# Moving the q casts of the later batches from ScalarE to GpSimd in a fused retention and MLP kernel

## The chip, the cores and the metric

The kernel runs on one core of a Trainium2 chip. The metric is the device time of one execution in microseconds (us). Each core has five engines with a queue of their own: TensorE (PE in the profile; PEld is its weight load), VectorE (DVE), ScalarE (ACT), GpSimd (POOL) and SyncE (SP, which here only issues DMAs). Batches are counted from 0, and a stage is named by the batch whose MLP runs in it.

## The reference, cut to what matters

Retention (a decayed linear attention, 4 batches, 8 heads, 768 positions, 64 per head) is followed by a Fourier mix, a normalization and a two-layer MLP with a residual.

```python
for t in range(S):                       # retention
    state = gamma * state + outer(k[:, :, t], v[:, :, t])
    y[:, :, t] = scale * q[:, :, t] @ state
x = y.transpose(0, 2, 1, 3).reshape(B, S, H * D)
u = x + real(fft(fft(x, axis=1), axis=2))
un = (u - mean(u)) / sqrt(var(u) + 1e-6)
out = u + relu(un @ w_ch1) @ w_ch2       # 512 -> 2048 -> 512
```

## The kernel before

The kernel does retention in chunks, two heads (a pair) at a time, four pairs per batch. It is a software pipeline: while the MLP of batch b runs on PE, the attention of batch b+1 is slipped in between its matmuls. For batches 2 and 3 each pair needs casts of q, k and v to fp16; q and k are then transposed by DMA. Before the change q is cast on ScalarE, k and v on GpSimd:

```python
def cast_unit(b, i):                     # batch b, pair i
    ...
        q16 = qzs[i % 2]                 # two q16z buffers, used in turn
        for h2 in range(2):
            dst = q16[:, h2, :, D * h2:D * h2 + D]
            nc.scalar.copy(dst, q32[:, h2])
    for h2 in range(2):
        kc = nc.gpsimd.tensor_scalar(out=kd[:, :, h2, :], in0=k32[:, h2],
                                     scalar1=gkd[...], scalar2=1.0, ...)
    last_cast[b, i] = nc.gpsimd.tensor_scalar(out=v16, in0=v32..., scalar1=1.0, scalar2=1.0, ...)
def t_unit(b, i):
    ...
    nc.sync.dma_start_transpose(qT, q16_of[b, i])   # q16z is free again when this has read it
    nc.sync.dma_start_transpose(kT, kd_of[b, i])
```

Beside the casts GpSimd has one more duty: it adds the residual x to u, per block of 128 rows, and VectorE's statistics (bn_stats, tile bst) wait for that:

```python
def s2_unit(b, kb):                      # row block kb of batch b, 0 to 5
    ...                                  # VectorE writes u from PSUM (pq) and qn
    nc.gpsimd.tensor_tensor(out=u[:, kb, 0:256], in0=u[:, kb, 0:256], in1=x..., op=ALU.add)
    nc.gpsimd.tensor_tensor(out=u[:, kb, 256:512], ...)
    nc.vector.bn_stats(bst, u[:, kb, :]) # then bn_aggr, and un on ScalarE
```

The MLP's first layer makes 16 row groups of psh in three PSUM buffers, which it shares with the second layer's psc. ScalarE or VectorE empties each psh into ht, by a list:

```python
def h_unit(b, rt, fb):
    psh = ps_pm.tile(...)                # three buffers
    ... four matmuls ...
    if fb in ACT_ROWS[rt]:
        nc.scalar.activation(ht16[:, fb, :], psh, AF.Relu, ...)
    else:
        nc.vector.tensor_scalar(out=ht16[:, fb, :], in0=psh, ...)
```

The other PSUM tiles of this phase share a pool of five buffers: wkA (q times k), wkK (v times k, for the state), wkY (the attention's output), pq (the Fourier mix) and pst (transposes of un).

Of the kernel before, what the change touches and what calls it, by code (L numbers as in the profile page):

```python
# [12 lines left out]
ALU = mybir.AluOpType  # L13
# [6 lines left out]
B, H, S, D = 4, 8, 768, 64  # L20
# [10 lines left out]
ON_ACT = {'q': (0, 1, 0), 'kv': (1, 1, 1), 'g': (0, 1, 1), 'gr': (0, 0, 0)}  # L31
FB = 1
NPE = 2
ACT_ROWS = ((2, 4, 5, 6, 7, 8, 9, 10, 14), (0, 3, 6, 7, 9, 10, 11, 12, 14, 15))


@with_exitstack
def kernel(
# [9 lines left out]
    nc = tc.nc  # L48
# [149 lines left out]
    for h in range(H):  # L198
# [4 lines left out]
                            scalar2=float(math.log(0.125)), op0=ALU.mult, op1=ALU.add)  # L203
    nc.vector.tensor_scalar(out=gexp[:, 1], in0=lgrow, scalar1=icol[:, 5:6], scalar2=None,
                            op0=ALU.mult)
    nc.scalar.activation(gexp, gexp, AF.Exp, bias=0.0, scale=1.0)
    for h2 in range(2):
# [10 lines left out]
                            scalar1=float(np.float32(1.0 / S)), scalar2=None, op0=ALU.mult)  # L218
    nc.vector.tensor_scalar(out=icoln[:, 3:5], in0=icol[:, 3:5], scalar1=float(1.0 / DM),
                            scalar2=None, op0=ALU.mult)  # L220
# [134 lines left out]
    def cast_unit(b, i):  # L355
        def run():
            h0 = 2 * PAIR_ORDER[i]
            q32, k32, v32 = (in_of.pop((n, b, i)) for n in "qkv")
            kd = kp.tile([P, NCH, 2, D], f16, tag="kd16", name="kd16")
            v16 = vp.tile([P, NCH, 2, D], f16, tag="v16", name="v16")  # L360
            with ExitStack() as es:
                if b < NPE:
                    if (b, i - 1) in last_cast:
                        es.enter_context(tc.issue_after(last_cast[b, i - 1].ins))
                    q16 = qzs[i % 2].rearrange("p h c d -> p (h c d)")[
                        :, 0:NCH * P].rearrange("p (c h d) -> p c h d", c=NCH, h=2)
                    es.enter_context(tc.issue_after(nc.gpsimd.tensor_scalar(
                        out=q16, in0=q32.rearrange("p h c d -> p c h d"), scalar1=1.0,
                        scalar2=1.0, op0=ALU.mult, op1=ALU.mult).ins))
                else:  # L370
                    q16 = qzs[i % 2]
                    for h2 in range(2):
                        dst = q16[:, h2, :, D * h2:D * h2 + D]
                        nc.scalar.copy(dst, q32[:, h2])
                for h2 in range(2):
                    kc = nc.gpsimd.tensor_scalar(out=kd[:, :, h2, :], in0=k32[:, h2],  # L376
                                                 scalar1=gkd[:, h0 + h2:h0 + h2 + 1],
                                                 scalar2=1.0, op0=ALU.mult, op1=ALU.mult)
                    if b < NPE:
                        es.enter_context(tc.issue_after(kc.ins))  # L380
                last_cast[b, i] = nc.gpsimd.tensor_scalar(
                    out=v16, in0=v32.rearrange("p h c d -> p c h d"), scalar1=1.0, scalar2=1.0,
                    op0=ALU.mult, op1=ALU.mult)
            q16_of[b, i], kd_of[b, i], v16_of[b, i] = q16, kd, v16
        return run
# [538 lines left out]
    def h_unit(b, rt, fb):  # L924
        def run():
            unT = lb[b]["unT"]
            psh = ps_pm.tile([P, 384], f32, tag="pm", name="psh", padded_shape=[P, DM])
            for cb in range(4):
                nc.tensor.matmul(psh, w116[:, cb, fb * P:(fb + 1) * P],  # L929
                                 unT[:, cb, rt * 384:(rt + 1) * 384],  # L930
                                 start=(cb == 0), stop=(cb == 3))
            if fb in ACT_ROWS[rt]:
                nc.scalar.activation(ht16[:, fb, :], psh, AF.Relu, bias=0.0, scale=-1.0)  # L933
            else:
                nc.vector.tensor_scalar(out=ht16[:, fb, :], in0=psh, scalar1=-1.0, scalar2=0.0,  # L935
                                        op0=ALU.mult, op1=ALU.max)
        return run
# [239 lines left out]
```

## Time and profile before

| | before |
|---|---|
| time, median of 4 runs (3 were known at the prediction, 249.08) | 248.9 us |
| span of the profiled run | 247.3 us |
| PE busy | 233.9 us (95%) |
| PE idle between 85 and 185 us | 2.4 us |
| stage of batch 1, first psh to first psc matmul | 95.02 to 109.04: 14.02 us |
| stage of batch 2, the same | 147.14 to 162.69: 15.55 us |

A stage holds the first half of the MLP's first layer and the casts and attention of the next batch, and both stages do the same work. So a stage's length, read from PE's timeline, shows a stall or a delay directly, with less noise than the time of a whole run; what noise is left, up to 0.4 us, is seen in batch 3's casts alone below.

### The profile page before, as it was taken

To read this page: it belongs to the slowest core of one execution; us is meant where nothing else is said; L and a number is where in the kernel's file an instruction comes from. 1 tells how busy PE (TensorE), PEld (TensorE's weight loads), DVE (VectorE), ACT (ScalarE), POOL (GpSimd) and SP (SyncE) were. 2 spreads that over 40 slices of the span, in tenths; PEclk is the share of its full clock that TensorE was granted. 3 is DMA by queue.
4 is the path that set the end of the run, shared out by engine and by line. 5 is a ranking of instruction groups with operands and counts; after the bars stand their busy time and mean duration, and the time that the engine had idled before them with its cause. 6 is when DMAs were issued, how large, how long until landed. Compare 5 with 4: busy or idle time off the path is not lost.

```text
span 247.3 us, 5310 instructions
## 1 busy us (share of the span) xinstructions
PE 233.9 (95%) x2024; PEld 144.0 (58%) x2024; DVE 176.2 (71%) x427; ACT 130.8 (53%) x295; POOL 73.7 (30%) x130
## 2 busy tenths in 40 slices
PE   6897899999999999999999999799999998999994
PEld 2454668956776645655567446465666455545543
DVE  8988957898788786995985738687895656424112
ACT  8798678487786437862247427742247317202500
POOL 6668500385500074660000717530001305000000
PEclk9999999999999999999999999999999999999999
DMA  8998999699999388999999479595200241221012
GB/s 174 259 257 142 200 197 205 155 248 260 271 229 211 55 170 182 202 168 162 226 265 210 102 156 201 111 127 130 87 1 3 44 150 21 45 85 42 0 45 85
DMA packets 99209, 36.39 MB, mean 147 GB/s; under 512 B 89840, under 2 KB 96240, under 8 KB 99184
## 3 DMA queue, kind: packets, MB, share of 16 engines
q1 hardware_dynamic: 94960, 31.86, 63.3%
q0 software_dynamic: 4224, 4.19, 10.5%
q8 instruction: 16, 0.26, 0.4%
q14 instruction: 9, 0.07, 0.1%
HBM read 27.26 MB, written 6.29 MB: 136 GB/s over the span
## 4 chain that ended last, share of the span: by engine, by line
PE 68%; DVE 10%; ACT 7%; POOL 4%; DMA 4%; SPq 3%; issue 2%; POOLq 0%; ACTq 0%; DVEq 0%
PE psc L972 30%; PE psh L929 20%; PE ps L729 3%; SPq L159 3%; PE psh L946 3%; DMA k<-in_k_dram 2%; PE wkA L593 2%; DMA qTz<-q16z 2%; DVE bst L882 2%; POOL u L865 2%; PE wkY L647 2%; ACT un L884 1%; DVE u L833 1%; PE wkY L643 1%; POOL u L863 1%
## 5 line engine op out<-in xcount | busy, mean ns | idle before, releaser
L972 PE MATMUL psc<-w,ht 128*128 128x512 f16 (+1 forms) x400 | 89.8, 370 | 0.0
L929 PE MATMUL psh<-unT,w 128*128 128x384 f16 x448 | 82.1, 326 | 2.3 <-ACT ht L933 2.2
L972 PEld LDWEIGHTS <-ht 128*128 128x128 f16 x400 | 38.0, 98 | 35.0
L929 PEld LDWEIGHTS <-w 128*128 128x128 f16 x448 | 42.2, 98 | 26.1 <-issue 3.3
L933 ACT ACTIVATE ht<-psh 128x384 f16<-128x384 f32 x67 | 31.9, 489 | 37.2 <-PE psh L929 36.2
L863 POOL TENSOR_TENSOR u<-u,x 128x256 f32<-128x256 f32 x21 | 13.3, 635 | 110.7 <-DVE u L833 100.3
L976 DVE SCALAR_TENSOR_TENSOR ob<-psc,stats,u 128x512 f32<-128x512 f32 (+1 forms) x25 | 18.0, 721 | 26.5 <-PE psc L972 26.4
L935 DVE TENSOR_SCALAR ht<-psh 128x384 f16<-128x384 f32 x45 | 24.7, 550 | 8.7 <-PE psh L929 8.2
L596 DVE TENSOR_TENSOR atm<-wkA,maskp 128x512 f16<-128x512 f32 x36 | 23.9, 682 | 1.0 <-PE wkA L593 1.0
L884 ACT ACTIVATE un<-u,stats 128x512 f16<-128x512 f32 x21 | 15.2, 723 | 15.2 <-DVE stats L883 10.9
L882 DVE BATCH_NORM_STATS2 bst<-u 128x6 f32<-128x512 f32 x21 | 14.6, 694 | 8.9 <-POOL u L865 8.8
L622 DVE SCALAR_TENSOR_TENSOR s<-s,gk,wkK 128x128 f16<-128x128 f16 x48 | 16.5, 343 | 2.5 <-ACT s L618 1.4
L655 ACT ACTIVATE x<-wkY,gexp 128x384 f16<-128x384 f32 x24 | 12.9, 584 | 8.3 <-PE wkY L647 8.3
L145 PE MATMUL wps<-ht 128*128 128x512 f16 x40 | 12.8, 422 | 2.2 <-POOL ht L196 2.2
L376 POOL TENSOR_SCALAR kd<-k,gexp 128x384 f16<-128x384 f32 x24 | 13.8, 585 | 2.2 <-DMA k<-in_k_dram 2.2
L865 POOL TENSOR_TENSOR u<-u,x 128x256 f32<-128x256 f32 x21 | 13.3, 635 | 3.6 <-DVE stats L883 1.8
L593 PE MATMUL wkA<-qTz,kT 128*128 128x256 f16 x72 | 13.6, 273 | 0.3 <-ACT x L655 0.2
L828 ACT COPY qn<-pq 128x128 f32<-128x128 f32 x18 | 4.9, 273 | 12.9 <-PE pq L826 12.9
L946 PE MATMUL psh<-unT,w 128*128 128x128 f16 x192 | 11.5, 219 | 0.1
L946 PEld LDWEIGHTS <-w 128*128 128x128 f16 x192 | 11.0, 98 | 0.7 <-issue 0.5
L833 DVE SCALAR_TENSOR_TENSOR u<-pq,g,qn 128x256 f32<-128x256 f32 x18 | 8.5, 474 | 3.1 <-ACT qn L829 2.8
L593 PEld LDWEIGHTS <-kT 128*128 128x128 f16 x72 | 6.7, 98 | 6.7 <-issue 0.9
(164 smaller groups left out, 319.1 us busy)
## 6 DMA issues: line engine op xcount, KB each, us to landing
q<-in_q_dram SPq DMA_DIRECT2D x16, 384.0 KB, 6.2
k<-in_k_dram SPq DMA_DIRECT2D x16, 384.0 KB, 5.6
v<-in_v_dram SPq DMA_DIRECT2D x16, 384.0 KB, 6.2
out_dram<-ob SPq DMA_DIRECT2D x23, 256.0 KB, 2.5
w<-in_moe_w_ch_dram POOLq DMA_DIRECT2D x8, 512.0 KB, 11.0
out_dram<-ob SPq DMA_DIRECT2D x2, 128.0 KB, 1.7
unT<-un SPq DMA_TRANSPOSE x15, 2.4
kT<-kd SPq DMA_TRANSPOSE x8, 3.1
```

What stands on the lines that cost most here:

```text
L593: mm = nc.tensor.matmul(wk[:, c2], st["kT"][:, c, :], st["qT"][:, :, c, :], start=True, stop=True)
L596: nc.vector.tensor_tensor(out=st["atm"][:, 2 * part:2 * part + 2], in0=wk, in1=maskp[:, PAIR_ORDER[i]].unsqueeze(1).to_broadcast([P, 2, 2, ...
L622: nc.vector.scalar_tensor_tensor(out=s16[:, c], in0=s16[:, c - 1], scalar=gk2[:, hp:hp + 1], in1=wk[:, c - c0], op0=ALU.mult, op1=ALU.add)
L865: nc.gpsimd.tensor_tensor(out=u[:, kb, 256:512], in0=u[:, kb, 256:512], in1=x[:, kb, 1, 257:1:-1], op=ALU.add)
L882: nc.vector.bn_stats(bst, u[:, kb, :])
L884: una = nc.scalar.activation(un, u[:, kb, :], AF.Identity, bias=stats[:, kb, 0:1], scale=-1.0)
L929: nc.tensor.matmul(psh, w116[:, cb, fb * P:(fb + 1) * P], unT[:, cb, rt * 384:(rt + 1) * 384], start=(cb == 0), stop=(cb == 3))
L933: nc.scalar.activation(ht16[:, fb, :], psh, AF.Relu, bias=0.0, scale=-1.0)
L935: nc.vector.tensor_scalar(out=ht16[:, fb, :], in0=psh, scalar1=-1.0, scalar2=0.0, op0=ALU.mult, op1=ALU.max)
L946: mm = nc.tensor.matmul(psh[:, f], w116[:, cb, fb * P:(fb + 1) * P], unT[:, cb, kb * P:(kb + 1) * P], start=(cb == 0), stop=(cb == 3))
L972: nc.tensor.matmul(psc[:, c0:c1], ht16[:, fb, rb3 * P:(rb3 + 1) * P], w216[:, fb, c0:c1], start=(fb == 0), stop=(fb == NFB - 1))
L976: nc.vector.scalar_tensor_tensor(out=ob[:, c0:c1], in0=psc[:, c0:c1], scalar=lb[b]["st"][:, rb, 3:4], in1=lb[b]["u"][:, rb, c0:c1], op0=AL ...
```

## The change

The intent: all casts of a pair stand in one queue, ScalarE is left to empty PSUM, and GpSimd, busy only 30%, takes the work.

```diff
-ACT_ROWS = ((2, 4, 5, 6, 7, 8, 9, 10, 14), (0, 3, 6, 7, 9, 10, 11, 12, 14, 15))
+ACT_ROWS = ((2, 4, 5, 6, 7, 8, 9, 10, 14), (0, 3, 6, 7, 9, 10, 11, 12, 14, 15), (2, 4, 5, 6, 7, 8, 9, 10, 14))
...
                         dst = q16[:, h2, :, D * h2:D * h2 + D]
-                        nc.scalar.copy(dst, q32[:, h2])
+                        nc.gpsimd.tensor_scalar(out=dst, in0=q32[:, h2], scalar1=1.0,
+                                                scalar2=1.0, op0=ALU.mult, op1=ALU.mult)
...
-            if fb in ACT_ROWS[rt]:
+            if fb in ACT_ROWS[2 if (b, rt) == (B - 1, 0) else rt]:
```

## The prediction

> **What bounds the kernel now.** I read the page first: how full TensorE (PE) is, and where.
>
> ```profile
> PE 233.9 (95%) x2024; PEld 144.0 (58%) x2024; DVE 176.2 (71%) x427; ACT 130.8 (53%) x295; POOL 73.7 (30%) x130
> PE   6897899999999999999999999799999998999994
> POOL 6668500385500074660000717530001305000000
> ```
>
> PE is busy 233.9 of 247.3 us. The missing 13.4 us lie mostly at the start and after the last matmul, so the table of busy time by stretch is needed: from 85 to 185 us, which holds everything the change touches, PE misses 0.49 us (85 to 100), 0.26 (100 to 115), 1.54 (145 to 160) and 0.09 (160 to 175), together 2.4 us or 1%. No change of casts can win more. GpSimd (POOL) has room on average (30%), but its strip has two crowded spells, near 87 to 110 and 140 to 163 us. The view of waits for PE between 85 and 185 us names the holes:
>
> ```profile
> PE psh L929 <- ACT ht L933: 1.5, 1, 1.5
> PE pst L913 <- ACT un L884: 0.4, 1, 0.4
> PE wkA L593 <- ACT x L655: 0.2, 1, 0.2
> ```
>
> One wait of 1.5 us is most of it: a matmul of the first MLP layer (psh) needs a PSUM buffer that ScalarE (ACT) has not emptied. The chain of work that ended last says why, and the timeline of ACT shows it directly:
>
> ```profile
> 150.85 5.25 DMA qTz<-q16z
> 156.20 0.17 ACT q16z L374
> 157.05 0.40 ACT q16z L374
> 157.45 0.39 ACT ht L933
> ```
>
> ```profile
> 156.20 0.51 ACT L374 CAST q16z<-q 128x384 f16<-128x384 f32 x1 [1.96 <-DMA qTz<-q16z]
> ```
>
> There are two q16z buffers. The cast of batch 3's fourth pair stands early in ACT's queue, and may not write its buffer before the transposing DMA of the second pair has read it, at 156.1. For 1.96 us ACT stands still, with PSUM to empty behind it, and PE stops:
>
> ```profile
> 155.92 0.44 PE L612 MATMUL wkK<-v,kd 128*128 128x128 f16 x5
> 157.90 0.81 PE L929 MATMUL psh<-unT,w 128*128 128x384 f16 x4 [1.54 <-ACT ht L933]
> ```
>
> The casts of batch 2 (counted from 0) run beside batch 1's MLP from 95 us on, those of batch 3 beside batch 2's from 147; below I name the stage by the MLP's batch. The earlier stage runs the same sequence without that stall: from the first psh matmul (95.02 and 147.14) to the second layer's first matmul (109.04 and 162.69) it takes 14.02 there and 15.55 here, 1.53 us more.
>
> **What the Trainium skill says.** "PSUM — Partial Sum Buffer", section "Engine vs sequencer instructions": the queues of ScalarE, VectorE and GpSimd are strict FIFO. The ACT stall agrees. "ScalarE: Activation LUTs", section "What ACT_TABLE_LOAD costs": an instruction with immediate scale and bias takes 186 ns + 0.833 ns per element, 506 ns for 384; the trace has 509 for the median q cast. "Perfetto Trace Analysis", section "GPSIMD Engine Instruction": GpSimd spans are unreliable, take the spacing of starts. I do so below; k casts listed at 1.15 us a pair are spaced 1.11. "GPSIMD Engine Reference", section "1. Specifications": GpSimd shares SBUF interfaces with VectorE, which contends in some forms. No number in this trace shows that, so I give it only width.
>
> **The change, part by part.** The third row list is a decoy: (2, 4, 5, ... 14) for the last batch's first half equals the list used now. The instruction order confirms it: PE's sequence is identical in both kernels. Value 0.
>
> Removed: 16 casts from ACT, 16 x 509 ns = 8.1 us of ACT's 130.8. ACT isn't the bound; what counts is the stall, 1.54 us of PE.
>
> Added: 16 casts on POOL. The nearest row is the k cast of the same shape and strides (585 ns, spacing 1.11 us for two), so 8 pairs x 1.11 = 8.9 us, POOL from 73.7 to about 83. That alone costs nothing. Where they stand does: in each pair q comes first, then k and v, and the residual additions of the next row block (u) follow in the same FIFO. POOL now, after batch 1's fourth row block:
>
> ```profile
> 98.20 0.64 POOL L865 TENSOR_TENSOR u<-u,x 128x256 f32<-128x256 f32 x1
> 98.82 1.15 POOL L376 TENSOR_SCALAR kd<-k,gexp 128x384 f16<-128x384 f32 x2
> 99.93 0.83 POOL L381 TENSOR_SCALAR v<-v 128x768 f16<-128x768 f32 x1
> 100.73 0.63 POOL L863 TENSOR_TENSOR u<-u,x 128x256 f32<-128x256 f32 x1
> 101.32 0.63 POOL L865 TENSOR_TENSOR u<-u,x 128x256 f32<-128x256 f32 x1
> ```
>
> There is no gap: with q in front, the additions of the fifth row block start at 101.84 and end near 103.1 instead of 101.95. VectorE (DVE) takes them at once, as its timeline shows, and it too is a FIFO:
>
> ```profile
> 102.01 0.68 DVE L882 BATCH_NORM_STATS2 bst<-u 128x6 f32<-128x512 f32 x1
> 105.70 0.54 DVE L935 TENSOR_SCALAR ht<-psh 128x384 f16<-128x384 f32 x1
> 106.86 0.55 DVE L935 TENSOR_SCALAR ht<-psh 128x384 f16<-128x384 f32 x1
> ```
>
> So the statistics move from 102.01 to about 103.13, and everything on DVE behind them, which is nearly gapless, by 1.12 us. That includes two evacuations of psh (rows 11 and 12 of 16), for which PE waits three rows later:
>
> ```profile
> 106.99 0.81 PE L929 MATMUL psh<-unT,w 128*128 128x384 f16 x4
> 107.85 0.81 PE L929 MATMUL psh<-unT,w 128*128 128x384 f16 x4
> ```
>
> Row 14 needs row 11's buffer, now free at 106.24, 0.75 us before. In the new DVE order one state update (spacing about 0.3 us) also steps ahead of that evacuation: it starts at 105.70 + 1.12 + 0.35 = 107.2 and ends at 107.75, so row 14 starts 0.8 us late. Row 12 follows after 0.47 for the evacuation and 0.62 for two updates, at 108.3 to 108.85; row 15 starts at 108.9, and the second layer, 0.87 us later, at 109.77 instead of 109.04: **+0.73 us** for batch 1.
>
> For batch 2 the stall goes, but the same delay comes in. Additions of the fifth block end at 155.38 instead of 154.27, the statistics start at 155.42; with batch 1's spacings the next u starts at 156.70, the next statistics at 158.49, row 11 is emptied at 159.51 to 160.05, row 14 starts at 160.1, row 15 at 161.2, the second layer at 162.07 instead of 162.69: **-0.62 us**.
>
> The other deadlines hold. Fourth-pair casts on POOL end near 112 and 164.6 (now 108.9 and 162.7), and the matmuls on that k and v come at 116.8 and 170.5. Their transposes are read at 121.2 and 174.9. Second pair in batch 1: k's transpose is issued 0.3 us later (102.4), read at 107.1, before row 14, so not in addition. Sum: +0.73 - 0.62 = **+0.1 us**, 249.2.
>
> **Rivals.**
> A, the pure gain: DVE and three PSUM buffers absorb POOL's delay, only the stall goes: 249.1 - 1.5 = 247.5. For it: the stall is certain to go from ACT, and ACT has 8 us less to do. Against: no gap on POOL ahead of the fifth block, and slack of only 0.75 us on row 11 against 1.5 us of delay.
> B, POOL becomes the local bound in both batches and transposes shift too: k's transpose of the second pair lands after 4.6 us already now, at 106.7 with PE right behind it, and one k load moves some 3 us later into that spell. Two losses of 1 us and a smaller gain: 250.3.
> C, the wait for the q16z buffer returns on POOL and holds k and v of the fourth pair. Against: by my times that cast starts after 109 and 159.7, its buffer is read out by 105 and 158. Worth 0.
>
> **Range and chances.** I give my sum about two thirds and A most of the rest: 0.65 x 249.2 + 0.25 x 247.5 + 0.1 x 250.3 = 248.9 us. From A with a little less (247.3) to B: 247.3 to 250.3. A gain of 2% would be 5 us, more than the 2.4 us that PE misses in the region; a loss of 2% needs several new stalls as large as the old one. Chances: faster 0.01, within 2% 0.97, slower 0.02.
>
> **What would show it.** Right: PE's wait of 1.5 us on ACT near 156 is gone; ACT is near 123 us busy, POOL near 83, its q casts as long as k casts; DVE waits about 1.1 us for POOL ahead of the fifth block's statistics (near 102 and 154.3); PE waits for DVE's ht near 107 and 159, under 1 us each. From psh to the second layer it takes about 14.8 us in both batches. Wrong, step by step: no PE wait on DVE there means A, and the delay was absorbed; a longer wait on k's transpose means B; a q cast on POOL much longer than 585 ns, or slower DVE instructions beside it, means that the two contend. A time below 247 or above 251 us would contradict the whole account.

## The result, and the profile after

The changed kernel takes 248.98 us (median of 4 runs, 248.76 to 249.18), the kernel before 248.9 (4 runs). The ratio is 1.0001, with a 95% interval of 0.9982 to 1.0019. Ratios here are the mean time of one kernel's runs over that of the other's runs of the same rounds, so they are not quite the ratio of the medians.

The page of the changed kernel, the same lines as shown of before (busy time of each engine, then busy tenths of PE and GpSimd in 40 slices):

```profile
PE 234.4 (95%) x2024; PEld 144.2 (58%) x2024; DVE 176.5 (71%) x427; ACT 124.8 (50%) x279; POOL 81.6 (33%) x146
PE   6797899999999999999999999999999998999994
POOL 7668500385500075690000636760002314000000
```

The work has moved: ACT lost 6.0 us of busy time, POOL gained 7.9. PE's strip has lost its 7 of the 26th slice (near 157 us), where the stall was, and is at 9 throughout from the sixth slice to the 33rd. Now the waits of PE between 85 and 185 us (engine, line and tile waited for: total us, times, longest):

```profile
PE wkY L644 <- DVE u L837: 0.8, 2, 0.4
PE pst L914 <- ACT un L885: 0.4, 1, 0.4
```

The 1.5 us wait on ScalarE is gone, and a new one has come that was not there: twice 0.4 us on VectorE's u. In the stage of batch 2 ScalarE no longer stops for the q16z buffer (it does wait 1.64 us for VectorE's statistics, before un at 157.23). Its timeline:

```profile
153.52 1.23 ACT L934 ACTIVATE ht<-psh 128x384 f16<-128x384 f32 x3
154.63 0.29 ACT L829 COPY qn<-pq 128x128 f32<-128x128 f32 x1
```

Before, the qn copy that follows these three evacuations came 3.6 us after their start (153.01 and 156.62), behind the stuck cast; now it comes 1.1 us after. So the stall is gone. What took the gain back shows in the chain of work that ended last, in the stage of batch 1 (start, duration, what; "..." marks what is left out):

```profile
99.79 1.13 POOL kd L377 x2
100.92 0.80 POOL v L382
101.73 0.60 POOL u L864
...
102.95 0.69 DVE bst L883
...
108.15 0.48 DVE ht L936
...
108.67 0.81 PE psh L930 x4
```

The chain now runs from GpSimd's casts over the additions and VectorE's statistics to a PSUM evacuation and into PE. Each link is the FIFO of one engine. The two groups on VectorE between 94 and 165 us that tell it, of before and then of the changed kernel (count | busy us, mean ns of one | idle before, ended by):

```profile
L882 DVE BATCH_NORM_STATS2 bst<-u 128x6 f32<-128x512 f32 x9 | 6.2, 692 | 3.2 <-POOL u L865 3.2
L596 DVE TENSOR_TENSOR atm<-wkA,maskp 128x512 f16<-128x512 f32 x18 | 12.0, 681 | 0.4 <-PE wkA L593 0.4
```

```profile
L883 DVE BATCH_NORM_STATS2 bst<-u 128x6 f32<-128x512 f32 x9 | 6.2, 694 | 5.0 <-POOL u L866 5.0
L597 DVE TENSOR_TENSOR atm<-wkA,maskp 128x512 f16<-128x512 f32 x18 | 12.0, 682 | 0.4 <-PE wkA L594 0.4
```

VectorE's instructions are no slower beside the added GpSimd work (692 and 694, 681 and 682 ns). It only waits 1.8 us longer for the additions, 0.9 in each stage. GpSimd's and VectorE's timelines give the size of the link: the q casts sit right ahead, and the statistics start at 102.95 where they had started at 102.01.

```profile
98.80 0.99 POOL L374 TENSOR_SCALAR q16z<-q 128x384 f16<-128x384 f32 x2
99.77 1.15 POOL L377 TENSOR_SCALAR kd<-k,gexp 128x384 f16<-128x384 f32 x2
```

```profile
102.95 0.69 DVE L883 BATCH_NORM_STATS2 bst<-u 128x6 f32<-128x512 f32 x1 [0.86 <-POOL u L866]
104.61 0.48 DVE L837 SCALAR_TENSOR_TENSOR u<-pq,g,qn 128x256 f32<-128x256 f32 x1
106.99 0.53 DVE L936 TENSOR_SCALAR ht<-psh 128x384 f16<-128x384 f32 x1
108.07 0.55 DVE L936 TENSOR_SCALAR ht<-psh 128x384 f16<-128x384 f32 x1
```

On PE, first in the stage of batch 1, then once in that of batch 2:

```profile
105.14 0.43 PE L644 MATMUL wkY<-s,qTz 128*128 128x64 f16 x9 [0.42 <-DVE u L837]
...
107.57 0.81 PE L930 MATMUL psh<-unT,w 128*128 128x384 f16 x4
...
157.97 0.44 PE L644 MATMUL wkY<-s,qTz 128*128 128x64 f16 x9 [0.42 <-DVE u L837]
```

PE first stops at wkY, whose PSUM buffer the late u frees at 104.61 + 0.48 = 105.09. Then row group 14 starts 0.05 us after VectorE has emptied row 11 (106.99 + 0.53 = 107.52), and row 15 starts at 108.67 (the chain's last line above), 0.05 us after row 12 is emptied (108.62). These two waits are real, too, though the view of waits does not list them. The stages now take 95.00 to 109.54 = 14.54 us and 147.64 to 162.36 = 14.72 us: +0.52 in the first, -0.83 in the second, -0.3 together, against a time that did not change within its noise (the rest of the span is 0.2 us longer).

### The profile page after: what moved, and what is told of

It is laid out like the page before. It is cut to its first block, busy times and chain, and to the rows that moved or that the text cites. A ratio compares the mean times of both kernels' runs of the same rounds, so it can differ in the third digit from the quotient of the medians.

```text
span 247.2 us, 5308 instructions
## 1 busy us (share of the span) xinstructions
PE 234.4 (95%) x2024; PEld 144.2 (58%) x2024; DVE 176.5 (71%) x427; ACT 124.8 (50%) x279; POOL 81.6 (33%) x146
## 4 chain that ended last, share of the span: by engine, by line
PE 66%; DVE 10%; POOL 8%; ACT 6%; SPq 3%; issue 2%; DMA 2%; POOLq 0%; DVEq 0%; ACTq 0%
PE psc L973 30%; PE psh L930 19%; PE ps L730 3%; SPq L159 3%; PE psh L947 3%; DVE bst L883 3%; POOL u L866 2%; DMA k<-in_k_dram 2%; POOL u L864 2%; PE wkA L594 2%; PE wkY L648 2%; DVE u L834 1%; DVE ht L936 1%; PE wkY L644 1%; PE tq L550 1%
## 5 line engine op out<-in xcount | busy, mean ns | idle before, releaser
L594 PE MATMUL wkA<-qTz,kT 128*128 128x256 f16 x72 | 13.6, 273 | 0.0
L382 POOL TENSOR_SCALAR v<-v 128x768 f16<-128x768 f32 x12 | 10.0, 833 | 2.0 <-DMA v<-in_v_dram 1.9
```

The costliest lines, as they stand in the source:

```text
L594: mm = nc.tensor.matmul(wk[:, c2], st["kT"][:, c, :], st["qT"][:, :, c, :], start=True, stop=True)
```

## The experiments

My theory is that two things of about the same size cancel. (1) In the stage of batch 2 the fourth pair's cast, waiting in ScalarE's queue for a buffer, costs some 1.5 us. (2) The second pair's q cast on GpSimd delays the additions of the fifth row block, and through VectorE's FIFO and the PSUM buffers it costs both stages. Rivals: the gain was hidden and nothing costs anything; GpSimd's added work costs in proportion, by contention or by sheer load; ScalarE's load, not its wait, is what mattered; VectorE's new instruction order is the loss. In all kernels PE's instructions stand in the same order; each result was correct. The order on ScalarE, casts aside, is not the same everywhere, and no run takes it apart: in batch 1's stage of the kernel before, of pair 2 alone and of batch 3's casts alone, the first emptying of wkY into x stands behind un and starts at 107.9 to 108.4 us; in all the others it stands ahead of un, at 104.9 to 106.9. In batch 2's stage the order is the same in all.

All runs together; "stage" is from the first psh to the first psc matmul in the profile, "rest" the span less both stages:

| run | time, median of 6 (of 4 for before, changed) | batch 1's stage | batch 2's stage | rest | ratio to before, 95% |
|---|---|---|---|---|---|
| before | 248.9 | 14.02 | 15.55 | 217.7 | |
| changed | 248.98 | 14.54 | 14.72 | 217.9 | 1.0001 (0.9982 to 1.0019) |
| pairs 3 and 4 on GpSimd | 247.21 | 13.91 | 13.73 | 217.5 | 0.9904 (0.9869 to 0.9940) |
| pair 2 alone | 249.51 | 14.35 | 15.88 | 217.7 | 0.9998 (0.9962 to 1.0034) |
| third buffer, casts on ScalarE | 247.40 | 13.55 | 13.61 | 217.9 | 0.9908 (0.9870 to 0.9946) |
| batch 2's casts alone | 248.91 | 14.52 | 15.04 | 217.5 | 0.9979 (0.9942 to 1.0016) |
| all but pair 2 on GpSimd | 246.99 | 13.57 | 13.75 | 217.5 | 0.9909 (0.9886 to 0.9931) |
| pair 2 cast twice | 251.62 | 15.70 | 15.88 | 217.7 | 1.0099 (1.0074 to 1.0125) |
| batch 3's casts alone | 248.71 | 14.38 | 14.70 | 217.6 | 0.9973 (0.9947 to 1.0000) |
| row list put back | 249.13 | 14.51 | 14.70 | 218.0 | 0.9995 (0.9972 to 1.0018) |

The rest stays within about 0.5 us everywhere, so differences larger than that lie in the two stages. The kernel before, run along, had medians of 249.62 (11 runs, 248.51 to 251.84) and 249.16 (248.37 to 250.29); differences of a few tenths are read from the stages, not from the ratios. I count pairs from 1 in this section; the code and the records' names count them from 0.

### Pairs 3 and 4 on GpSimd, pairs 1 and 2 on ScalarE

```diff
+                        if i >= 2:
                             nc.gpsimd.tensor_scalar(out=dst, ...)
+                        else:
+                            nc.scalar.copy(dst, q32[:, h2])
```

> Only the q casts of the third and fourth head pair go to GpSimd; those of the first and second stay on ScalarE. My theory (the stall of 1.5 us comes from the fourth pair's cast waiting in ScalarE's queue, the loss from the second pair's cast standing ahead of the fifth block's additions on GpSimd): both stages run without PE waits over 0.3 us, 14.0 us from the first psh to the first psc matmul in each, and the time is 248.9 - 1.5 = 247.4 us. Rival (GpSimd's extra work costs in proportion, whichever pair it is): half of the change's loss stays, some 248.4 us. Rival (the stall was hidden anyway): 248.9.

Measured 247.21 us, 13.91 and 13.73 us. Half of the casts moved, and the time is below the 247.4 of my theory and the proportional rival's 248.4. The stall wasn't hidden: without it and without the delay the time falls. Against the kernel before in the same rounds the gain is 2.4 us (0.9904), more than the 1.5 expected: the kernel before ran slower in these rounds (249.62) than its 248.9, and, as the third buffer shows below, its stage of batch 1 was not clean either.

### Pair 2 alone on GpSimd

The condition is `i == 1` instead of `i >= 2`.

> Only the second pair's q cast goes to GpSimd. My theory: the fifth block's additions are delayed by 0.97 us as in the changed kernel; in batch 1's stage PE loses about 0.5 us (14.5 instead of 14.0 us); in batch 2's stage the old stall of 1.5 us stays and covers the delay; 248.9 + 0.5 = 249.4 us. Rival (cost in proportion to GpSimd's work): a quarter of the loss, 249.15. Rival (the loss comes from the new order of VectorE's instructions, which this kernel does not have): 14.0 us in batch 1's stage and 248.9.

Measured 249.51 us. The ratio cannot resolve 0.5 us, since before's own runs scattered that day. The profile can. PE's waits between 85 and 185 us have both causes at once:

```profile
PE psh L933 <- ACT ht L937: 1.8, 2, 1.5
PE wkY L647 <- DVE u L840: 0.4, 1, 0.4
```

The wkY wait comes with this one pair, and with VectorE's instructions in before's order, so the new order is not its cause. Batch 1's stage is 14.35 us, 0.33 longer, less than the 0.5 expected. In batch 2's stage I had expected the stall to cover the delay; it did not quite, 15.88 instead of 15.55. The trace says why. The second pair's cast on GpSimd ends later, so its transpose is issued at 152.33 instead of 150.85, and the fourth pair's cast on ScalarE gets its buffer at 156.73 instead of 156.20:

```profile
152.33 1.43 SPq L545 DMA_TRANSPOSE qTz<-q16z  x1
156.73 0.51 ACT L378 CAST q16z<-q 128x384 f16<-128x384 f32 x1 [2.29 <-DMA qTz<-q16z]
```

That is 0.53 us later, in a stage that began 0.20 us later (147.34): the 0.33 us. The run also shows that two casts fewer in ScalarE's queue do not remove the stall: PE still waits 1.45 us at 158.01.

### A third q16z buffer, all q casts on ScalarE

From the kernel before, not the changed one. The third buffer lies in part of a table that only batch 0 reads; the middle lines are the loop that zeroes the buffers' padding.

```diff
+    qzs.append(gk5[:, 1:4].rearrange("p n e c -> p (n e c)").bitcast(f16)[
+        :, 0:2 * NCH * P].rearrange("p (h c d) -> p h c d", h=2, c=NCH))
...
-        for j in range(2):
+        for j in range(3):
...
-                    q16 = qzs[i % 2]
+                    q16 = qzs[(0, 1, 0, 2)[i]]
```

> All q casts stay on ScalarE as before, but the fourth pair's goes to a third q16z buffer (in memory that only batch 0 uses), so that it has no transpose to wait for. My theory (the wait, not ScalarE's 8 us of casts, cost the 1.5 us): no ScalarE wait on the transpose, stages of 14.0 and about 14.1 us, 247.4 us. Rival (ScalarE's load is what held PE): the stage of batch 2 keeps over 15 us and the time stays at 248.9.

Measured 247.40 us. That this is the expected number to the digit is luck: the two stages are 0.9 us shorter than I had expected, and against the kernel before in the same rounds the gain is 2.3 us (0.9908) and not 1.5. ScalarE keeps all of its 16 casts and its wait on the transpose is gone, and both stages are the shortest of all with 13.55 and 13.61 us. The edit moved something else too: with its own buffer the fourth pair's cast stands much earlier in ScalarE's queue (143.58 us instead of 156.20), so the stage of batch 2 holds two casts less. That this load is not what mattered is shown by pair 2 alone, where two other casts left the same stage and the stall stayed. Together the two runs show that the wait for the buffer cost the time in batch 2's stage. This also corrects my ruler: batch 1's 14.02 us before was not clean, an undisturbed stage takes about 13.6. How much of that half microsecond is ScalarE's order (x behind un) and how much the landing of transposes is not shown.

### Batch 2's casts alone on GpSimd

The condition is `b == 2`.

> Only batch 2's q casts go to GpSimd (they run beside batch 1's MLP, where there was no stall to remove); batch 3's stay on ScalarE. My theory: loss without gain, batch 1's stage 14.5 us, batch 2's 15.5 as before, 249.4 us. Rival (the change costs nothing by itself and its gain is hidden too): 248.9.

Measured 248.91 us, a miss by 0.5. The first half of the expectation holds: batch 1's stage takes 14.52 us. But batch 2's fell from 15.55 to 15.04 with its casts on ScalarE as before. The stall itself, from PE's timeline, is shorter than the 1.54 us of before, and the times of the second pair's transpose and of the fourth pair's cast behind it say how:

```profile
151.28 1.48 SPq L545 DMA_TRANSPOSE qTz<-q16z  x1
155.94 0.51 ACT L378 CAST q16z<-q 128x384 f16<-128x384 f32 x1 [1.45 <-DMA qTz<-q16z]
157.64 0.81 PE L933 MATMUL psh<-unT,w 128*128 128x384 f16 x4 [1.02 <-ACT ht L937]
```

PE reaches this stage 0.25 us later than before (first psh at 147.39 instead of 147.14), because of the delay in the stage of batch 1. The second pair's cast comes later with it (150.16 for 149.91), and its transpose is issued at 151.28 for 150.85. But from there to the fourth pair's cast it took 4.66 us and not 5.35 (156.20 - 150.85). These 0.69 us, less the 0.18 by which the issue came later within the stage, are the 0.51 us that the stage lost (15.55 to 15.04). So the delay did not vanish into the stall, since the issue moved with it; the transpose was quicker in this profile. In pair 2 alone it took 4.40 us (152.33 to 156.73). What makes it quicker or slower is left open. The theory's loss is seen in batch 1's stage; in the whole time it is not.

### All but pair 2 on GpSimd

The condition is `i != 1`.

> The changed kernel with only the second pair's q cast put back on ScalarE; three of four pairs stay on GpSimd. My theory: the loss is all in that pair, so three quarters of GpSimd's new work cost nothing: 247.3 us, as with two pairs on GpSimd, both stages 13.6 to 14.0 us. Rival (cost in proportion to the casts on GpSimd): between 247.2 (two pairs) and 249.0 (four pairs), near 248.1. It also has the changed kernel's order on VectorE; if that order cost anything, it would show as a stage over 14.2 us.

Measured 246.99 us, stages of 13.57 and 13.75 us. Three quarters of the casts on GpSimd cost nothing that shows (with all on ScalarE and a third buffer the stages took 13.55 and 13.61), and one pair makes 2.0 us of difference to the changed kernel (248.98; 2.1 us to the last experiment below, which has the same instructions and ran in the same rounds). Each stage is 0.97 us shorter than the changed kernel's, the spacing of the two q casts. PE, VectorE, ScalarE and GpSimd all have the changed kernel's order here, the q casts aside, so this is the cleanest comparison. Between 85 and 185 us one PE wait is left, and VectorE's statistics follow without a gap:

```profile
PE pst L917 <- ACT un L888: 0.4, 1, 0.4
```

```profile
101.76 0.69 DVE L886 BATCH_NORM_STATS2 bst<-u 128x6 f32<-128x512 f32 x1
```

This falsifies the rivals of proportion, of contention and of VectorE's order together, and it has the lowest median, 0.9% below the kernel before, though it cannot be told from pairs 3 and 4 on GpSimd (0.9904) and the third buffer (0.9908), whose intervals overlap with its own.

### Pair 2 cast twice on GpSimd

```diff
+                        for _ in range(2 if i == 1 else 1):
                             nc.gpsimd.tensor_scalar(out=dst, ...)
```

> The changed kernel with the second pair's q cast done twice on GpSimd (same result). My theory: the fifth block's additions come another 0.97 us later in both stages; the buffers' slack is spent already, so nearly all of it reaches PE: stages of some 15.5 and 15.7 us instead of 14.5 and 14.7, 249.0 + 1.9 = 250.9 us, 250.0 at the least. Rival (the delay of these additions is absorbed, the loss has another source): 249.0.

Measured 251.62 us, 0.7 above my number, stages of 15.70 and 15.88 us: 1.16 more in each than in the changed kernel. PE's waits (85 to 185 us) and VectorE's wait for the additions:

```profile
PE wkY L645 <- DVE atm L598: 1.5, 2, 0.8
PE wkY L645 <- DVE u L838: 1.3, 2, 0.7
```

```profile
103.87 0.69 DVE L884 BATCH_NORM_STATS2 bst<-u 128x6 f32<-128x512 f32 x1 [2.04 <-POOL u L867]
```

VectorE waits 2.04 us instead of 0.86, that is 1.18 more, because the doubled pair took 2.15 us from start to start (98.55 to 100.70) and a single one 0.97. All 1.16 us reach PE: past the first cast there is no slack left. My 0.97 for the second cast was too small by 0.2.

### Batch 3's casts alone on GpSimd

The condition is `b == 3`.

> Only batch 3's q casts go to GpSimd. My theory: batch 1's stage 13.6 to 14.0 us as before, batch 2's 14.7 as in the changed kernel, so 248.9 - 0.8 = 248.1 us. Rival (the change is neutral in each stage by itself): 248.9.

Measured 248.71 us (247.57 to 249.12), between both numbers. Batch 2's stage, 14.70 us, is what the theory says. Batch 1's, which this kernel does not change, took 14.38 us in the profiled run. Its extra waits are for the transposed k and for a PSUM buffer behind ScalarE's x:

```profile
PE wkA L597 <- DMA kT<-kd: 0.4, 1, 0.4
PE wkA L597 <- ACT x L659: 0.2, 1, 0.2
```

With q on ScalarE the second pair's k transpose lands just when PE needs it. Batch 1's stage so varies between 13.55 and 14.38 us among kernels that cast batch 2's second pair on ScalarE, and the same kernel's time varies by 1.5 us from run to run. Since 14.02 and 14.38 us belong to the same instructions in that stage, the ruler itself is uncertain by some 0.4 us there, as much as pair 2 alone added to it (0.33); that loss rests on the wkY wait seen in its trace and on the comparison of the changed kernel with all but pair 2. The wait for x comes with ScalarE's order: here and in the kernel before, x stands behind un (108.42 and 108.20 us); the kernels with x ahead of un do not have this wait. What sets the transpose's landing is left open.

### The row list put back

```diff
-            if fb in ACT_ROWS[2 if (b, rt) == (B - 1, 0) else rt]:
+            if fb in ACT_ROWS[rt]:
```

> The changed kernel with the list of ACT rows put back. Its instructions stand in the same order on every engine as the changed kernel's, so it must run in the same time, 249.0 us; what it differs by is the noise of these runs, which I expect below 0.3 us.

Measured 249.13 us, stages equal to the changed kernel's within 0.03 us. The added list does nothing, and 0.15 us is the difference between two runs of the same instructions.

## Why the prediction was right, point by point

- **The bound and its ceiling**: right. PE is the bound, and its idle time in 85 to 185 us set the scale of everything. In the best version the two stages together are 2.25 us shorter than before.
- **The row list**: right, shown by the instruction order and the last run.
- **The stall on ScalarE**: right, and shown by the third buffer and by pairs 3 and 4 on GpSimd, which end it, and by pair 2 alone, which takes as much load off ScalarE's stage as the third buffer does and keeps it.
- **The delay over GpSimd's and VectorE's FIFOs**: right in kind, shown by taking pair 2 out (-2.0 us) and by doubling it (+2.6 us; -2.1 and +2.5 against the run of the same instructions in the same rounds). Mis-sized is the term for the two q casts: they are spaced 0.97 us, not the 1.11 of the k casts, so the statistics moved by 0.94 us and not by 1.12. With that the losses came out 0.2 us smaller in each stage: +0.52 for +0.73, and -0.83 for -0.62.
- **Which wait PE meets first**: missed. I followed the psh evacuations. They do hold PE (rows 14 and 15 start at 107.57 and 108.67, predicted 107.8 and 108.9), but before them the late u holds a buffer of the other PSUM pool, and wkY stops 0.42 us. It lies within the same delay, so the sum did not suffer.
- **The reference of 14.02 us as a clean stage**: wrong. It held about half a microsecond of other waits; an undisturbed stage takes 13.6. Against that the delay costs 0.97 us in each stage and the old stall, with what followed from it, almost 2. The predicted difference was hardly touched by it: the working took 0.87 us from row 15 to the second layer, where the kernel before had 1.19 (107.85 to 109.04), so it had left that wait out.
- **Rivals**: A, the absorbed delay, is what the kernel would do without pair 2, not what it does. B's late k transpose exists, but as jitter of the kernels with q on ScalarE, not as a loss of the change. C was worth 0, as said.
- **Busy times**: GpSimd 81.6 for about 83 predicted, since q casts take 0.51 us and not 0.585; ScalarE 124.8 for about 123, since neighbouring instructions overlap and busy time counts the overlap once. The prediction's 506 ns for a q cast on ScalarE is an estimate from the formula that it cites, which the page gives for ACTIVATE; the trace, which names these instructions CAST, has 509.
- **The centre**: 248.9 predicted, 248.98 measured; the sum of the working alone was 249.2. That the weighted centre came so close is luck: the stages gave -0.3 us where the working said +0.1, and the time did not follow the stages within its noise.

## What to carry to other kernels

When work moves to a half-idle engine, the question is what stands behind it in that engine's queue at that moment, and how soon somebody waits for it; here 0.97 us ahead of one addition gave back a gain that three other pairs kept. A change that measures zero can hold two effects worth keeping apart: undo it part by part, with a ruler shorter than the whole run. A stall for a buffer can be cured where it is, by another buffer, without moving any work.

## What the Trainium skill lacked or had wrong

- "GPSIMD Engine Reference", section "4.1 Engine selection", calls one-input work roughly line-rate and has no figure for a cast with a per-partition scalar against constants. Here a 128x384 cast from fp32 to fp16 took 513 ns with two constants and 587 ns with a per-partition scalar, spaced 0.97 and 1.12 us for two.
- "Perfetto Trace Analysis", section "Optimization Strategy", says to find the gaps on the most-contended engine and what blocks them. The gaps that the view of waits listed understated what there was to gain: the changed kernel shows 0.8 us of PE waits on VectorE between 85 and 185 us, and taking their cause away made the two stages 1.94 us shorter. Only the stages of both kernels laid side by side showed that.
